# Scores of split f16 pairs from half the array's rows, without stacked copies, and a third input buffer

## The chip, the cores and the metric

The kernel runs on one core of one Trainium2 chip. A core has a matrix engine (TensorE, PE in the profile, with its weight loads shown apart as PEld), a vector engine (VectorE, DVE), a scalar engine (ScalarE, ACT), a general engine (GpSimd, POOL), and a queue engine (SyncE, SP) that here issues nearly all transfers. The metric is the device time of one execution in microseconds, the median of several.

## What is computed

```python
# q, k, v: (8, 12, 448, 64); w_in: (768, 2048); w_out: (2048, 768); all float32
scores = q @ k.T / sqrt(64) - log(448)
attn   = 1 / (1 + exp(-scores))            # sigmoid, no row sums
x      = attn @ v                          # heads side by side: (3584, 768)
h      = x @ w_in
g      = where(h >= 1, h, where(h <= -1, 0, (h + 1)**2 / 4))
out    = g @ w_out
```

## The kernel before

The work is cut by batch (8 of them, 448 tokens each). In a batch the 12 heads make 6 pairs of heads, so there are 48 pairs, counted p = 0 to 47. The two heads of a pair lie in partitions 0 to 63 and 64 to 127, since a head is 64 wide. A pair's keys are cut into chunks of 128: three whole ones and a last one of 64, in which both heads share one tile (`mid` in the code).

**Pairs and their formats.** Pairs 0 to 7 are computed in float32 straight from the input. From pair 8 on, q and k are split into a high and a low f16 part (from pair 14 on v and the sigmoids too), and a score is the sum of three terms: high by high, low k by high q, high k by low q. A pair passes these steps: `load_pair` transfers its q, k and v into a tile `raw` (704 KB, lines 304 to 321); `prep_a` lets ACT sum absolute values of q, k and v for a scale (line 337; the tile `dump` receives what nobody reads); `all_sum` adds the sums over partitions (line 154 and a small matmul, line 157); `prep_b` makes scales on DVE and splits the tile, on POOL from pair 17 on, into `hl` (for q and k, each high and low) and `v` (lines 373 to 375). The last reader of a `raw` tile is the split of its v on line 375.

**The stacked copy.** `prep_b` then copies `hl` into a tile `qk` by 8 transfers of 56 KB: for each head, high q stands twice, in rows 0 to 63 and 64 to 127, and high k above low k. A matmul over all 128 rows (line 443) then gives the first two terms of one head at once; the third term is a matmul over a head's own 64 rows (line 458). The transfers go through SP's queue, which is in order, and each waits for the part of the split that it copies. The last chunk of pairs 14 and later is done otherwise, by three matmuls with a block of `corner` weights (line 436).

**The rest of attention.** ACT makes the sigmoid in place (line 487), ACT and DVE split it (lines 495 and 496), and PE multiplies with v (line 533). The result of the pair is taken from PSUM by ACT (line 542), its largest value by DVE (line 543).

**The two products.** Batches 0 and 1 use plain f16 splits of `w_in` (line 761). From batch 2 on the product with `w_in` is done in blocks with seven products in place of eight (line 727), with sums in between on ACT and DVE (lines 739, 736 and 745). `bend` makes g: ACT (line 774), DVE twice (775 and 776), ACT writes the high part of g to `ghl` (777), DVE the low part (778). The product with `w_out` (line 797) reads `ghl`, chunk by chunk; its tile `po` is scaled by DVE (line 810) and stored. `load_set` (line 703) brings the next blocks of weights. I call the first product of a batch the up blocks and the second the down products. The g of the last up block is ready only some time after PE has gone on to the down products.

**Order.** The attention of batch b + 1 is woven into the products of batch b: `step(i)` handles a chunk, and its first chunk of a pair p calls `load_pair(p + 3)` and `prep_a(p + 2)`, its third chunk `prep_b(p + 2)` and, from pair 14 on, `prep_a(p + 3)`. The program text gives priorities only; a scheduler with a simulated timeline puts each engine's instructions in order, and each engine then works in that order and waits at the first instruction that isn't ready. The tile `raw` has two buffers, so pair p + 3 can be loaded only when pair p + 1 has been split.

```python
        if c == 0:
            load_pair(p + 3)
            prep_a(p + 2)
        if c == 2:
            prep_b(p + 2)
            if late:
                prep_a(p + 3)
```

Of the kernel before, what the change touches and what calls it, by code (L numbers as in the profile page):

```python
# [14 lines left out]
F32 = mybir.dt.float32  # L15
F16 = mybir.dt.float16
# [7 lines left out]
P = 128  # L24
# [7 lines left out]
NFULL = 8  # L32
NHALF = 6
# [38 lines left out]
def sigmoid_attention_mlp(ctx: ExitStack, tc: tile.TileContext, first_qvk, qkv, w_in, w_out, out_t):  # L72
    nc = tc.nc
    NFULL, _, _, S = first_qvk.shape
# [3 lines left out]
    D = P // 2  # L78
    VW = S + D
    NKC = S // P  # L80
    NPC = NKC + 1
# [5 lines left out]
    raw_p = ctx.enter_context(tc.tile_pool(name="raw", bufs=2))  # L87
    stk_p = ctx.enter_context(tc.tile_pool(name="stk", bufs=2))
# [31 lines left out]
    rows = xhl.rearrange("p c h n -> p (c h n)").bitcast(F32)  # L120
    blocks = drm_p.tile([NFC // 2, P, SET], F16, name="blocks")

    def scales(m, n, tag, pool=None, square=False, less=0):
# [24 lines left out]
        out=ident, in_=ident, pattern=[[-1, P]], compare_op=ALU.is_equal, fill=0.0, base=0, channel_multiplier=1  # L148
# [136 lines left out]
    raws, maxes, ready, hls, sums = {}, {}, {}, {}, {}  # L285
# [7 lines left out]
    def slot_of(p):  # L293

        return (p + 2) % NFB
# [8 lines left out]
    def load_pair(p):  # L304
        if p >= NPAIR or not first_time("load", p):
            return
        if p < NFULL:
            r = full[:, slot_of(p)]
            nc.sync.dma_start(out=r[:, ::2, :], in_=first_qvk[p, :, ::2, :])
            nc.sync.dma_start(out=r[:, 1, :], in_=first_qvk[p, :, 1, :])  # L310
            ready[p] = r, r[:, 1]
            return
        src = qkv[p - NFULL]
        raws[p] = raw_p.tile([P, 2 * S + VW], F32, tag="raw", name="raw")
        if p < NFULL + NHALF:
            v = stk_p.tile([P, VW], F32, tag="v", name="v", bufs=3)
            nc.sync.dma_start(out=raws[p][:, : 2 * S], in_=src[:, : 2 * S])
            nc.sync.dma_start(out=v, in_=src[:, 2 * S :])
            ready[p] = v
        else:  # L320
            nc.sync.dma_start(out=raws[p], in_=src)
# [22 lines left out]
    def prep_b(p):  # L344
        if not NFULL <= p < NPAIR or not first_time("split", p):
            return
        r, m = raws.pop(p), maxes.pop(p)
        n = 2 if p < NFULL + NHALF else 3
        m = sums.pop(p) if p in sums else all_sum(m, n)

        s, inv = scales(m, n, "qkv")
        sqk = sml_p.tile([P, 2], F32, tag="sqk", name="sqk")
        if n == 3:
            nc.vector.tensor_scalar(out=sqk[:, 1:2], in0=inv[:, 2:3], scalar1=1.0 / ATT, scalar2=None, op0=ALU.mult)
        nc.vector.tensor_scalar(
            out=sqk[:, 0:1], in0=inv[:, 0:1], scalar1=inv[:, 1:2], scalar2=1.0 / math.sqrt(D), op0=ALU.mult, op1=ALU.mult
        )
        hl = hls.pop(p, None) or stk_p.tile([P, 2, 2, S], F16, tag="hl", name="hl")
        parts = [hl[:, 0], hl[:, 1]]
        if n == 3:  # L360
            v = stk_p.tile([P, 2, VW], F16, tag="v", name="v", bufs=3)
            parts.append(v)
        else:
            v = ready[p]
        for t, dst in enumerate(parts):
            rt, hi = r[:, t * S : 2 * S + VW if t == 2 else (t + 1) * S], dst[:, 0, :]
            if p < QA and t != QT:
                nc.scalar.activation(hi, rt, AF.Copy, scale=s[:, t : t + 1])
                nc.vector.scalar_tensor_tensor(  # L369
                    out=dst[:, 1, :], in0=rt, scalar=s[:, t : t + 1], in1=hi, op0=ALU.mult, op1=ALU.subtract  # L370
                )
                continue
            nc.gpsimd.tensor_scalar(out=rt, in0=rt, scalar1=s[:, t : t + 1], scalar2=1.0, op0=ALU.mult, op1=ALU.mult)  # L373
            nc.gpsimd.tensor_scalar(out=hi, in0=rt, scalar1=1.0, scalar2=1.0, op0=ALU.mult, op1=ALU.mult)
            nc.gpsimd.tensor_tensor(out=dst[:, 1, :], in0=rt, in1=hi, op=ALU.subtract)  # L375

        qk = stk_p.tile([P, 2, 2, S], F16, tag="qk", name="qk")
        for j in range(2):
            src = slice(j * D, (j + 1) * D)
            for h in range(2):  # L380
                dst = slice(h * D, (h + 1) * D)
                nc.sync.dma_start(out=qk[dst, j, 0], in_=hl[src, 0, 0, :])
                nc.sync.dma_start(out=qk[dst, j, 1], in_=hl[src, 1, h, :])
        ready[p] = qk, v, sqk, inv, hl

    pieces = {}

# [16 lines left out]
    def chain():  # L404

        begun = []

        def run(issue):
            if not begun:
                begun.append(issue())  # L410
                return
            with tc.high_priority(offset=RUN_PRIO):
                tc.keep_in_program_order(issue())

        return run

    def scores(todo):

        tiles = []
        for i in todo:  # L420
            p, c = divmod(i, NPC)
            mid = c == NKC
            w = slice(c * P, S if mid else (c + 1) * P)
            psc = ps_sc.tile([P, 2, 512], F32, tag="psc", name="psc")
            tiles.append(psc)
            run = chain()
            if p < NFULL:
                r = ready[p][0]
                for j in range(2):
                    out = psc[j * D : (j + 1) * D, 0, :S] if mid else psc[:, j, :S]  # L430
                    rows = slice(j * D, (j + 1) * D)
                    run(lambda: nc.tensor.matmul(out, r[rows, 2, w], r[rows, 0, :], start=True, stop=True))
            elif mid and p >= NFULL + NHALF:
                hl = ready[p][4]
                for t, (kh, qh) in enumerate(((0, 0), (1, 0), (0, 1))):
                    run(lambda: nc.tensor.matmul(
                        psc[:, 0, :S], corner(p)[:, kh, :], hl[:, 0, qh, :], start=t == 0, stop=t == 2
                    ))
            else:
                kq = ready[p][0]  # L440
                for j in (1, 0):
                    out = psc[j * D : (j + 1) * D, 0, :S] if mid else psc[:, j, :S]
                    run(lambda: nc.tensor.matmul(out, kq[:, j, 1, w], kq[:, j, 0, :], start=True, stop=False))  # L443
        for i, psc in zip(todo, tiles):
            p, c = divmod(i, NPC)
            if c == NKC and p >= NFULL + NHALF and p + 2 in maxes:

                sums[p + 2] = all_sum(maxes[p + 2], 3, psc[:, 1, :])
        for i, psc in zip(todo, tiles):
            p, c = divmod(i, NPC)  # L450
            mid = c == NKC
            if p >= NFULL and not (mid and p >= NFULL + NHALF):
                hl, w = ready[p][4], slice(c * P, S if mid else (c + 1) * P)
                run = chain()
                for j in range(2):
                    rows = slice(j * D, (j + 1) * D)
                    out = psc[rows, 0, :S] if mid else psc[:, j, :S]
                    run(lambda: nc.tensor.matmul(out, hl[rows, 1, 0, w], hl[rows, 0, 1, :], start=False, stop=True))  # L458
        for i, psc in zip(todo, tiles):
            weigh(i, psc)  # L460
        for p, c in (divmod(i, NPC) for i in todo):
            if c == 0 and p >= NFULL + NHALF:
                if p < NFULL + NHALF + 2:
                    nc.gpsimd.memset(corner(p), 0.0)
                for j in range(2):
                    rows = slice(j * D, (j + 1) * D)
                    (nc.vector if p < CORN else nc.gpsimd).tensor_copy(  # L467
                        out=corner(p)[rows, :, rows], in_=ready[p][4][rows, 1, :, NKC * P :]
                    )

    def corner(p):

        return corners[:, p % 2 * 2 * P : (p % 2 + 1) * 2 * P].rearrange("p (h n) -> p h n", h=2)
# [359 lines left out]
    def step(i):  # L833

        p, c = divmod(i, NPC)
        late = i >= NPC * (NFULL + NHALF)
        if c == 0:
            load_pair(p + 3)
            prep_a(p + 2)
        if c == 2:  # L840
            prep_b(p + 2)
            if late:
                prep_a(p + 3)
        if i < NPC * GROUPED:
            more, some = i + LAG + 1, [i]
        else:

            more, some = i + 4, [i, i + 1]
            if c % 2:
                return  # L850
        more = min(more, B * NPIECE)
        if more > state["scored"]:
            scores(range(state["scored"], more))
            state["scored"] = more
        av(some)
# [155 lines left out]
```

## Time and profile before

| | |
|---|---|
| median of 3 runs | 1168.32 us (1165.77 to 1192.78) |
| the profiled execution | 1167.41 us, of which its span 1165.40 us |
| PE busy | 1124.0 us, 96% |
| DVE busy | 820.0 us, 70% |
| ACT busy | 723.3 us, 62% |
| POOL busy | 295.6 us, 25% |
| transfers | 170.00 MB, of which `qk` 320 of 56 KB each |

The span counts from the first instruction to the last. Busy times of PE are those of overlapping matmuls: a matmul of 448 columns is shown with about 355 ns, but the next one starts 189 ns after it. In the views below, a row of the timeline gives start, duration and engine, then source line, operation, tile written and tiles read, and the count of instructions that were merged; in square brackets stands how long the engine had been idle before it and what ended that. A row of the chain of waits is shorter: start, duration, engine, tile and line. PEclk is the granted share of the matrix engine's clock.

### The profile page before, as it was taken

To read this page: it belongs to the slowest core of one execution; us is meant where nothing else is said; L and a number is where in the kernel's file an instruction comes from. 1 tells how busy PE (TensorE), PEld (TensorE's weight loads), DVE (VectorE), ACT (ScalarE), POOL (GpSimd) and SP (SyncE) were. 2 spreads that over 40 slices of the span, in tenths; PEclk is the share of its full clock that TensorE was granted. 3 is DMA by queue.
4 is the path that set the end of the run, shared out by engine and by line. 5 is a ranking of instruction groups with operands and counts; after the bars stand their busy time and mean duration, and the time that the engine had idled before them with its cause. 6 is when DMAs were issued, how large, how long until landed. Compare 5 with 4: busy or idle time off the path is not lost.

```text
span 1165.4 us, 20217 instructions
## 1 busy us (share of the span) xinstructions
PE 1124.0 (96%) x7662; PEld 670.0 (57%) x7662; DVE 820.0 (70%) x1730; ACT 723.3 (62%) x1199; POOL 295.6 (25%) x367
## 2 busy tenths in 40 slices
PE   8899999999999999999999998999999998999998
PEld 2234334544446874577645875467845676558954
DVE  6988877778877993569835897268954689636820
ACT  6978887568758884568644786448854576423410
POOL 0000000001552362325432443415354233310000
PEclk9999999999999999999999999999999999999999
DMA  9943442252555654235622464214733064302300
GB/s 361 381 138 138 158 150 88 58 199 88 202 186 188 246 195 134 65 131 207 214 65 65 140 239 166 75 55 158 271 128 100 28 235 146 109 24 105 150 19 30
DMA packets 58112, 170.00 MB, mean 146 GB/s; under 512 B 8608, under 2 KB 39840, under 8 KB 51872
## 3 DMA queue, kind: packets, MB, share of 16 engines
q1 hardware_dynamic: 56288, 159.29, 39.5%
q10 hardware_dynamic: 1728, 9.44, 2.2%
q8 instruction: 60, 0.98, 0.3%
q14 instruction: 36, 0.29, 0.1%
HBM read 126.94 MB, written 23.40 MB: 129 GB/s over the span
## 4 chain that ended last, share of the span: by engine, by line
PE 65%; DVE 14%; ACT 6%; DMA 5%; POOL 4%; issue 4%; SPq 1%; POOLq 0%; ACTq 0%; DVEq 0%
PE po L797 31%; PE ph L727 14%; PE ph L761 7%; PE pav L533 6%; DMA raw<-qkv 4%; DVE ahl L496 3%; PE psc L443 3%; DVE g L775 2%; DVE g L776 2%; DVE xhl L736 2%; PE psc L458 2%; POOL hl L375 2%; DVE ghl L778 1%; POOL raw L373 1%; DMA w_out_sb<-w_in 1%
## 5 line engine op out<-in xcount | busy, mean ns | idle before, releaser
L797 PE MATMUL po<-ghl,w_out_sb 128*128 128x448 f16 x2304 | 451.9, 355 | 10.7 <-ACT ghl L777 10.2
L797 PEld LDWEIGHTS <-w_out_sb 128*128 128x128 f16 x2304 | 222.8, 98 | 228.9 <-issue 30.5
L727 PE MATMUL ph<-w_in_sb 128*128 128x224 f16 x3024 | 306.7, 260 | 9.8 <-DVE xhl L736 8.6
L727 PEld LDWEIGHTS <-w_in_sb 128*128 128x128 f16 x3024 | 285.7, 98 | 33.0 <-issue 26.5
L496 DVE SCALAR_TENSOR_TENSOR ahl<-psc,ahl 128x896 f16<-128x896 f32 (+1 forms) x170 | 152.8, 899 | 119.1 <-ACT ahl L495 117.5
L487 ACT ACTIVATE psc<-psc,nls,sqk 128x896 f32<-128x896 f32 (+1 forms) x136 | 129.9, 969 | 93.6 <-PE psc L458 57.7
L373 POOL TENSOR_SCALAR raw<-raw,qkv_s 128x448 f32<-128x448 f32 (+1 forms) x93 | 68.6, 752 | 439.8 <-DVE qkv_i L137 248.0
L495 ACT ACTIVATE ahl<-psc 128x896 f16<-128x896 f32 (+1 forms) x170 | 127.9, 762 | 35.1 <-DVE ahl L496 33.3
L761 PE MATMUL ph<-xhl,w_in_sb 128*128 128x448 f16 x576 | 112.5, 353 | 2.1 <-DVE g L776 2.1
L337 ACT ACTIVATE dump<-raw 128x448 f16<-128x448 f32 (+1 forms) x105 | 61.6, 587 | 71.1 <-DMA raw<-qkv 67.0
L778 DVE TENSOR_TENSOR ghl<-g,ghl 128x448 f16<-128x448 f32 x128 | 85.8, 677 | 23.1 <-ACT ghl L777 22.7
L736 DVE TENSOR_TENSOR xhl<-ph,xhl 128x224 f32<-128x224 f32 x240 | 87.1, 382 | 15.9 <-PE ph L727 11.4
L777 ACT ACTIVATE ghl<-g 128x448 f16<-128x448 f32 x128 | 73.2, 573 | 34.3 <-DVE g L776 33.4
L774 ACT ACTIVATE g<-xhl,hr,ihr 128x448 f32<-128x448 f32 x96 | 68.4, 753 | 38.9 <-DVE xhl L736 38.1
L775 DVE SCALAR_TENSOR_TENSOR g<-g,rk 128x448 f32<-128x448 f32 x112 | 85.2, 774 | 9.2 <-ACT g L774 8.8
L761 PEld LDWEIGHTS <-w_in_sb 128*128 128x128 f16 x576 | 54.9, 98 | 59.8 <-issue 9.9
L533 PE MATMUL pav<-ahl,v 128*64 128x448 f16 x748 | 83.7, 357 | 2.3 <-DVE ahl L496 2.3
L375 POOL TENSOR_TENSOR hl<-raw,hl 128x448 f16<-128x448 f32 x62 | 72.8, 1195 | 0.0
L776 DVE SCALAR_TENSOR_TENSOR g<-xhl,ihs,g 128x448 f32<-128x448 f32 x96 | 72.0, 770 | 0.2
L443 PE MATMUL psc<-qk 128*128 128x448 f16 x252 | 65.1, 354 | 2.8 <-ACT a L484 1.6
L810 DVE TENSOR_SCALAR o<-po,od 128x448 f32<-128x448 f32 x42 | 28.5, 678 | 55.2 <-PE po L797 55.1
L467 POOL COPY w_in_sb<-hl 64x128 f16<-64x128 f16 x68 | 32.7, 480 | 134.9 <-DVE hl L369 133.0
(151 smaller groups left out, 1122.7 us busy)
## 6 DMA issues: line engine op xcount, KB each, us to landing
w_in_sb<-blocks SPq DMA_DIRECT2D x48, 1344.0 KB, 6.4
raw<-qkv SPq DMA_DIRECT2D x34, 704.0 KB, 5.0
qk<-hl SPq DMA_DIRECT2D x320, 56.0 KB, 2.0
w_out_sb<-w_in SPq DMA_DIRECT2D x16, 768.0 KB, 11.1
out_t<-o SPq DMA_DIRECT2D x48, 224.0 KB, 1.9
blocks<-mixs SPq DMA_DIRECT2D x8, 768.0 KB, 3.8
w_out_sb<-w_out ACTq DMA_DIRECT2D x6, 768.0 KB, 5.0
raww<-w_out ACTq DMA_DIRECT2D x6, 768.0 KB, 5.3
```

What stands on the lines that cost most here:

```text
L375: nc.gpsimd.tensor_tensor(out=dst[:, 1, :], in0=rt, in1=hi, op=ALU.subtract)
L443: run(lambda: nc.tensor.matmul(out, kq[:, j, 1, w], kq[:, j, 0, :], start=True, stop=False))
L487: nc.scalar.activation(a, a, AF.Sigmoid, bias=nls, scale=sqk)
L495: nc.scalar.activation(hi, x, AF.Copy, scale=ATT)
L496: made.setdefault(i, []).append(nc.vector.scalar_tensor_tensor(out=lo, in0=x, scalar=ATT, in1=hi, op0=ALU.mult, op1=ALU.subtract))
L533: run(lambda: once(nc.tensor.matmul(pav[j * D : (j + 1) * D, :S], *terms[j][t], start=c == 0 and t == 0, stop=mid and t == len(terms[j]) - ...
L727: nc.tensor.matmul(out, w[:, wt, wh, c * P : (c + 1) * P], xc[:, xt, c, xh, :], start=j in (0, 2) and c + wh + xh == 0, stop=c == HC - 1 a ...
L736: add = lambda out, q, other: nc.vector.tensor_tensor(out=out, in0=quarter(q), in1=other, op=ALU.add)
L761: nc.tensor.matmul(ph[:, :S], w_in_sb[:, f, wh, c * P : (c + 1) * P], xhl[:, c, xh, :], start=c == 0 and wh + xh == 0, stop=c == NCC - 1 a ...
L775: nc.vector.scalar_tensor_tensor(out=g, in0=g, scalar=rt, in1=g, op0=ALU.min, op1=ALU.mult)
L778: (nc.gpsimd if f % GPOOL else nc.vector).tensor_tensor(out=ghl[:, f, 1, :], in0=g, in1=hi, op=ALU.subtract)
L797: nc.tensor.matmul(po[:, :S], w_out_sb[:, f, wh, m * P : (m + 1) * P], ghl[:, f, gh, :], start=f == lo and wh + gh == 0, stop=f == hi - 1 ...
```

## The change

The stacked copy is gone, with its tile and its 8 transfers per pair. All three terms of a chunk are matmuls over a head's own 64 rows, straight from `hl`, in six instructions: both heads' first term, both heads' second, both heads' third. The last chunk of pairs 8 to 13 is done likewise with 64 rows and 64 columns; that of later pairs stays with `corner`. `raw` has three buffers in place of two, and from pair 15 on a pair's load is called one pair sooner.

```diff
-        raws[p] = raw_p.tile([P, 2 * S + VW], F32, tag="raw", name="raw")
+        raws[p] = raw_p.tile([P, 2 * S + VW], F32, tag="raw", name="raw", bufs=3)
...
-        qk = stk_p.tile([P, 2, 2, S], F16, tag="qk", name="qk")
-        for j in range(2):
-            src = slice(j * D, (j + 1) * D)
-            for h in range(2):
-                dst = slice(h * D, (h + 1) * D)
-                nc.sync.dma_start(out=qk[dst, j, 0], in_=hl[src, 0, 0, :])
-                nc.sync.dma_start(out=qk[dst, j, 1], in_=hl[src, 1, h, :])
-        ready[p] = qk, v, sqk, inv, hl
+        ready[p] = hl, v, sqk
...
-                kq = ready[p][0]
-                for j in (1, 0):
-                    out = psc[j * D : (j + 1) * D, 0, :S] if mid else psc[:, j, :S]
-                    run(lambda: nc.tensor.matmul(out, kq[:, j, 1, w], kq[:, j, 0, :], start=True, stop=False))
+                hl = ready[p][0]
+                for t, (kh, qh) in enumerate(((0, 0), (1, 0), (0, 1))):
+                    for j in range(2):
+                        rows = slice(j * D, (j + 1) * D)
+                        out = psc[rows, 0, :S] if mid else psc[:, j, :S]
+                        run(lambda: nc.tensor.matmul(
+                            out, hl[rows, 1, kh, w], hl[rows, 0, qh, :], start=t == 0, stop=t == 2
+                        ))
...
-        for i, psc in zip(todo, tiles):
-            p, c = divmod(i, NPC)
-            mid = c == NKC
-            if p >= NFULL and not (mid and p >= NFULL + NHALF):
-                hl, w = ready[p][4], slice(c * P, S if mid else (c + 1) * P)
-                run = chain()
-                for j in range(2):
-                    rows = slice(j * D, (j + 1) * D)
-                    out = psc[rows, 0, :S] if mid else psc[:, j, :S]
-                    run(lambda: nc.tensor.matmul(out, hl[rows, 1, 0, w], hl[rows, 0, 1, :], start=False, stop=True))
...
             load_pair(p + 3)
+            if p + 4 > NFULL + NHALF:
+                load_pair(p + 4)
             prep_a(p + 2)
```

The scheduler makes a new order of it. Two places carry the prediction. The first is SP, in batch 3, around the load that the ACT rows further down wait for. Before, where `raw_6310` is pair 31, `qk_6190<-hl_6179` the copies of pair 29, and `w_in_sb<-blocks` the next weights:

```order
L321 DMA raw_6047<-qkv 128x1408
L703 DMA w_in_sb_90<-blocks_95 128x5376 x2
L382 DMA qk_6190<-hl_6179 64x448
L383 DMA qk_6190<-hl_6179 64x448
L382 DMA qk_6190<-hl_6179 64x448 x2
L383 DMA qk_6190<-hl_6179 64x448 x2
L382 DMA qk_6190<-hl_6179 64x448
L383 DMA qk_6190<-hl_6179 64x448
L321 DMA raw_6310<-qkv 128x1408
L703 DMA w_in_sb_90<-blocks_95 128x5376
L812 DMA out_t<-o_6279 128x448
```

Now, at the same place on SP, where `raw_5990` is pair 31 and `raw_6250` pair 32 (L690 is the old line 703, L799 the old 812):

```order
L321 DMA raw_5697<-qkv 128x1408
L690 DMA w_in_sb_90<-blocks_95 128x5376 x2
L321 DMA raw_5990<-qkv 128x1408
L690 DMA w_in_sb_90<-blocks_95 128x5376 x2
L321 DMA raw_6250<-qkv 128x1408
L690 DMA w_in_sb_90<-blocks_95 128x5376
L799 DMA out_t<-o_6219 128x448
```

The copies are gone, and each load's place holds the next pair: pair 32 now stands where pair 31 stood. Pair 32 takes the third buffer, which pair 29 had; pair 31 took pair 29's buffer before.

The second place is ACT, in the same batch, where the last up blocks' g goes to the first down products. Before, from the last first step of `bend` on (L774) to the writing of `ghl` (L777), with the sums of absolute values of pair 31 (L337):

```order
L774 ACTIVATE g_6272<-xhl_93,hr0_5093,ihr0_5091 128x448
L337 ACTIVATE dump_6430,m3_6429<-raw_6310 128x448
L777 ACTIVATE ghl_94<-g_6266 128x448
L337 ACTIVATE dump_6430,m3_6429<-raw_6310 128x448
L777 ACTIVATE ghl_94<-g_6272 128x448
L487 ACTIVATE psc_6312<-psc_6312,nls_87,sqk_5891 128x2x448
L337 ACTIVATE dump_6430,m3_6429<-raw_6310 128x512
```

Now (L761 is the old line 774, L764 the old 777, L474 the old 487):

```order
L761 ACTIVATE g_6212<-xhl_93,hr0_5045,ihr0_5043 128x448
L337 ACTIVATE dump_6363,m3_6362<-raw_5990 128x448 x2
L337 ACTIVATE dump_6363,m3_6362<-raw_5990 128x512
L764 ACTIVATE ghl_94<-g_6206 128x448
L337 ACTIVATE dump_6562,m3_6561<-raw_6250 128x448
L764 ACTIVATE ghl_94<-g_6212 128x448
L474 ACTIVATE psc_6252<-psc_6252,nls_87,sqk_5839 128x2x448
L337 ACTIVATE dump_6562,m3_6561<-raw_6250 128x448
```

All three sums of pair 31 now stand ahead of both writings of `ghl`, and the first sum of pair 32 stands between the two. The same rows, with the pairs of that batch, stand in batches 2 to 5.

More of the change, by code (lines that the diff above doesn't have):

```diff
@@ L433, in scores @@
             elif mid and p >= NFULL + NHALF:
-                hl = ready[p][4]
+                hl = ready[p][0]
                 for t, (kh, qh) in enumerate(((0, 0), (1, 0), (0, 1))):
@@ L439, in scores @@
             else:
-                kq = ready[p][0]
-                for j in (1, 0):
-                    out = psc[j * D : (j + 1) * D, 0, :S] if mid else psc[:, j, :S]
-                    run(lambda: nc.tensor.matmul(out, kq[:, j, 1, w], kq[:, j, 0, :], start=True, stop=False))
+                hl = ready[p][0]
+                for t, (kh, qh) in enumerate(((0, 0), (1, 0), (0, 1))):
[5 more added lines that the diff above has]
+                        ))
         for i, psc in zip(todo, tiles):
@@ L467, in scores @@
                     (nc.vector if p < CORN else nc.gpsimd).tensor_copy(
-                        out=corner(p)[rows, :, rows], in_=ready[p][4][rows, 1, :, NKC * P :]
+                        out=corner(p)[rows, :, rows], in_=ready[p][0][rows, 1, :, NKC * P :]
                     )
```

## The prediction

> **What bounds the kernel now.** I read the page first, then who waits for whom, then the timeline where the long waits are.
>
> ```profile
> PE 1124.0 (96%) x7662; PEld 670.0 (57%) x7662; DVE 820.0 (70%) x1730; ACT 723.3 (62%) x1199; POOL 295.6 (25%) x367
> PE po L797 <- ACT ghl L777: 10.2, 4, 2.9
> PE ph L727 <- DVE xhl L736: 8.6, 7, 2.6
> ACT dump L337 <- DMA raw<-qkv: 67.0, 15, 7.0
> ```
>
> PE is the bound: of 1165.4 us it idles 41. The waits (total, times, longest) say what a change of inputs can reach. ACT stands still 67.0 us for `raw`, but only what arrives at PE counts. The largest entry there is the down product waiting four times, 10.2 us, for ACT's `ghl`. The timeline of one of the four, in batch 3, tells why (last SP copies and the load, POOL's last split, DVE, ACT, PE, and the transfer from the chain of waits):
>
> ```profile
> 573.28 1.16 POOL L375 TENSOR_TENSOR v<-raw,v 128x512 f16<-128x512 f32 x1
> 574.49 0.60 SPq L383 DMA_DIRECT2D qk<-hl  x1
> 575.19 0.53 SPq L321 DMA_DIRECT2D raw<-qkv  x1
> 575.19 5.12 DMA raw<-qkv
> 576.23 1.27 DVE L776 SCALAR_TENSOR_TENSOR g<-xhl,ihs,g 128x448 f32<-128x448 f32 x2
> 572.82 1.41 ACT L774 ACTIVATE g<-xhl,hr,ihr 128x448 f32<-128x448 f32 x2 [1.00 <-DVE xhl L736]
> 580.39 0.58 ACT L337 ACTIVATE dump<-raw 128x448 f16<-128x448 f32 x1 [6.16 <-DMA raw<-qkv]
> 580.97 0.56 ACT L777 ACTIVATE ghl<-g 128x448 f16<-128x448 f32 x1
> 581.99 0.56 ACT L777 ACTIVATE ghl<-g 128x448 f16<-128x448 f32 x1
> 577.82 2.06 PE L797 MATMUL po<-ghl,w_out_sb 128*128 128x448 f16 x10
> 582.61 8.54 PE L797 MATMUL po<-ghl,w_out_sb 128*128 128x448 f16 x36 [2.72 <-ACT ghl L777]
> ```
>
> Both g are ready on DVE at 576.23 + 1.27 = 577.5, but ACT stands in front of a sum for pair 31, whose `raw` lands at 575.19 + 5.12 = 580.31. It was issued late since it waits for pair 29's split on POOL (end 574.44) and for the last copies. The second `ghl` is there at 582.55, and PE starts at 582.61.
>
> The wait costs more than its length. These are the same 36 products after each of the four waits (chain of waits), and PEclk behind two of them:
>
> ```profile
> 444.53 6.97 PE po L797 x36
> 722.49 8.57 PE po L797 x36
> 861.47 8.65 PE po L797 x36
> 1111.39 50.33 PE po L797 x266
> 444.00:447.00 3.00, 2.47 (x14) 1.28 (x14) 0.91 (x3) 3.00 (x7) 0.00 (x0) 1.00 0.11 39
> 582.00:586.00 4.00, 3.40 (x10) 1.41 (x10) 1.39 (x4) 3.99 (x8) 0.00 (x0) 0.57 0.02 8
> ```
>
> At full clock the 36 take 6.97 us (50.33 / 266 = 0.189 each), after three of the waits 8.54, 8.57 and 8.65: 1.57 + 1.60 + 1.68 = 4.85 us lost to a granted clock of 0.57 over those windows. The Trainium skill ("TensorE: Matmul & The Clock Gate", Why this matters for your kernels) asks for no idle gap over some 3 us; here 2.72 us of idling was enough at 582 and 2.46 was not at 444, so the measured rows decide.
>
> **The scores on PE.** The timeline has both kinds of matmul next to each other, for two chunks and for one:
>
> ```profile
> 507.20 0.92 PE L443 MATMUL psc<-qk 128*128 128x448 f16 x4
> 508.05 0.55 PE L458 MATMUL psc<-hl 64*128 64x448 f16 x4
> 508.53 0.76 PE L533 MATMUL pav<-ahl,v 128*64 128x448 f16 x6
> 513.93 0.54 PE L443 MATMUL psc<-qk 128*128 128x448 f16 x2
> 514.40 0.36 PE L458 MATMUL psc<-hl 64*128 64x448 f16 x2
> 514.70 1.90 PE L727 MATMUL ph<-w_in_sb 128*128 128x224 f16 x18
> ```
>
> Two half-row matmuls take 514.70 - 514.40 = 0.30, four take 508.53 - 508.05 = 0.48. So a second pair of them costs 0.18, as much as one full matmul: the two halves run side by side, and about 0.11 is a change between array shapes. A whole chunk was two full slots and one shared by two halves, three slots; now it is three shared slots, three again. 0.77 us (513.93 to 514.70) stays about 0.77. What grows: the last chunk of pairs 8 to 13, where the two heads' first matmuls had 64 columns each, side by side, goes from two slots to three, 6 x 0.19 = 1.1 us. And by the new order PE changes its array shape 417 times, counted through, where it did 404 times; 13 x 0.1 = 1.3 us. Together +2.4.
>
> **The transfers.** 320 copies leave SP and the DMA engines:
>
> ```profile
> qk<-hl SPq DMA_DIRECT2D x320, 56.0 KB, 2.0
> raw<-qkv SPq DMA_DIRECT2D x34, 704.0 KB, 5.0
> ```
>
> No row of PE's waits names `qk`, so the copies themselves give nothing. What counts is `raw`. One would expect the sums never to wait again, as each load is a pair ahead. The order says otherwise at the four places: pair 31's three sums stand ahead of the `ghl` and find their tile loaded long before; but the scheduler has moved up pair 32's first sum too, between the two `ghl`, and pair 32's load waits for the same split of pair 29, at the same place on SP. On SP only the copies in front are gone. So the load goes out at 574.5 in place of 575.19, lands at 579.6; the sum takes 0.58 and the second `ghl` 0.56, and PE can go on at about 580.9. It arrives at 577.82 + 10 x 0.189 = 579.7. The wait shrinks from 2.9 to 1.2, 1.7 saved, four times: 6.8 us. Pair 31's own sums (1.8 us after 574.23) end before the first g is ready at 576.9, so they cost nothing. Waits of 1.2 us left the clock alone in this trace, for example here (batch 3, up blocks; 36 at 0.096 and a tail make 3.6):
>
> ```profile
> 552.41 3.61 PE L727 MATMUL ph<-w_in_sb 128*128 128x224 f16 x36 [1.06 <-DVE xhl L736]
> 984.99 5.27 PE L727 MATMUL ph<-w_in_sb 128*128 128x224 f16 x36 [1.25 <-DVE xhl L736]
> ```
>
> I count the 4.85 us of clock as saved too. The second row shows the exception: behind several waits in a row the same 36 took 1.66 more. Its waits begin with `raw` of pair 47, which DVE sums itself:
>
> ```profile
> 953.72 0.39 SPq L321 DMA_DIRECT2D raw<-qkv  x1
> 961.35 1.68 DVE L341 TENSOR_REDUCE m<-raw 128x2 f32<-128x896 f32 x2 [3.46 <-DMA raw<-qkv]
> 966.30 1.89 PE L727 MATMUL ph<-w_in_sb 128*128 128x224 f16 x18 [2.61 <-DVE xhl L736]
> ```
>
> Here the new load stands a whole pair earlier on SP and needs the buffer of pair 44, split long before, so the 2.61 us go in full. Of the 1.66 behind it I take half, 0.8 (bounds 0 and 1.66). Two waits around 300 us follow an ACT stopped by `raw`:
>
> ```profile
> 304.58 0.58 ACT L337 ACTIVATE dump<-raw 128x448 f16<-128x448 f32 x1 [1.81 <-DMA raw<-qkv]
> 309.35 1.14 PE L533 MATMUL pav<-ahl,v 128*64 128x448 f16 x10 [1.25 <-DVE ahl L496]
> 325.38 0.58 ACT L337 ACTIVATE dump<-raw 128x448 f16<-128x448 f32 x1 [1.33 <-DMA raw<-qkv]
> 332.99 1.14 PE L533 MATMUL pav<-ahl,v 128*64 128x448 f16 x10 [1.08 <-DVE ahl L496]
> ```
>
> Of 1.25 + 1.08 = 2.3 I take half, 1.2, since mixing of weights fills ACT there too. The new order of everything else has no row. The nearest is the wait of 1.06 at 552.41, which stands in each of four batches: it can go (-4.2) or come twice (+4.2). I see no reason for either side and take 0. SP's waits for a free `raw` stay where they were, so the weight loads and output stores behind them are no later.
>
> The sum: 2.4 - 6.8 - 4.85 - 2.6 - 0.8 - 1.2 = -13.9. From the profiled 1167.41 that is 1153.5; the median lies 0.9 above the profiled execution, so I forecast 1154.
>
> **Rivals.** *The stall stays.* The sum moved up by the scheduler stands in the same line as before; if its transfer takes 1 us longer, or POOL ends pair 29's split 1 us later, the wait at the down products is over 2 us again and the clock drops as at 861.47. Then the 6.8 mostly and the 4.85 are not saved: 1153.5 + 11.7 = about 1165, no change. For it: the same split releases the load. Against: the copies in front are gone, and only one sum stands between.
>
> *Half-row weights don't load ahead* (the side of slower). If the next weights of a half could be loaded only when that half's matmul is done, each following pair of halves pays a weight load.
>
> ```profile
> L458 PEld LDWEIGHTS <-hl x252: 92/92/103, 78.2 to 1023.3; 64*128 64x128 f16 x120, 64*64 64x64 f16 x6
> ```
>
> There are 126 such chunks (120 whole, 6 short) with two following pairs each, 252 x 0.092 = 23.2 us: 1177. It decides from 0.06 us per following pair on, where it eats the 13.9. The Trainium skill ("TensorE: Matmul & The Clock Gate", Part 3, The mechanism) states just this rule: a weight load overlaps matmuls in flight only in other row groups, and here every second load is for the row group that is computing. The four halves at 508.05 speak against it, since their second pair came 0.18 after the first.
>
> *All waits on these chains go.* If landing is quick enough, the left 4 x 1.2 go too, and with them the 1.06 of four batches and the other halves of the small terms: 1154 - 4.8 - 4.2 - 2.0 = 1143.
>
> **How the numbers follow.** The forecast has 0.52, the stall that stays 0.25 (between 1160 and 1168), all waits gone 0.12 (1143 to 1149), weights not ahead 0.07, a new wait of another kind 0.04 (1168 to 1175). By itself the forecast's range is 1149 to 1160. The range 1147 to 1168 leaves out the slow ends and part of the fastest. What can be told from no change in a measurement of this kernel is some 2%, 23 us: under 1145 lies a part of the third case, 0.05; over 1191.7 next to nothing, 0.02; the rest, 0.93, is within.
>
> **What would show it.** ACT's total wait for `raw` falls from 67 us to 10 or 15, with four waits of some 2 us left at the turn to the down products; PE waits for `ghl` there about 1.2 us each, and 36 products take 7.0 after each. Pairs of half-row matmuls start 0.19 apart. DVE's wait for pair 47 is gone. I am wrong if PEclk still falls near 0.57 at those places, if a whole chunk takes over 0.9 us on PE, or if the waits of the up blocks grow.

## The result, and the profile after

| | before | after |
|---|---|---|
| median | 1168.68 us of 4 | 1154.53 us of 4 (1152.82 to 1156.25) |
| the profiled execution | 1167.41 us, span 1165.40 | 1152.84 us, span 1151.1 |
| ratio | | 0.9887 [0.9856, 0.9918] |
| transfers | 170.00 MB | 151.64 MB |

The kernel is 1.1% faster, which is less than the 2% that this measurement tells from no change; the interval alone keeps it under 1. The forecast was 1154. One execution of before (1192.78 us) and one of the first experiment below (1912.69 us) were slow ones; the ratios leave them out, and without them the medians of these two kernels are 1168.32 and 1165.00 us. Line numbers are now 13 lower behind the scores: L784 is the old down product L797, L714 the old up block L727, L764 the old `ghl` L777. L438 are the new scores, L429 is the old `corner` line 436.

The busy times of the page of after come first, and its row for the sums of absolute values on ACT; then the first entry of who waits for whom on PE (total, times, longest, in us):

```profile
PE 1120.0 (97%) x7914; PEld 660.7 (57%) x7914; DVE 831.4 (72%) x1730; ACT 721.2 (63%) x1199; POOL 291.3 (25%) x367
L337 ACT ACTIVATE dump<-raw 128x448 f16<-128x448 f32 (+1 forms) x105 | 61.5, 586 | 2.7 <-DVE mb L154 1.3
PE ph L714 <- DVE xhl L723: 10.5, 6, 3.2
```

ACT's wait for `raw`, 67.0 us before, is gone altogether: 2.7 us of idling are left ahead of its sums, and none of it for a transfer. The down products no longer wait for ACT's `ghl` (10.2 us before). The largest entry left for PE is a wait for DVE. The timeline of after at the turn in batch 3, to be laid beside the one in the prediction (POOL, SP, ACT, PE):

```profile
571.68 1.53 POOL L375 TENSOR_TENSOR v<-raw,v 128x512 f16<-128x512 f32 x1
573.24 0.33 SPq L321 DMA_DIRECT2D raw<-qkv  x1
578.47 0.56 ACT L337 ACTIVATE dump<-raw 128x448 f16<-128x448 f32 x1
579.03 0.56 ACT L764 ACTIVATE ghl<-g 128x448 f16<-128x448 f32 x1
577.24 9.25 PE L784 MATMUL po<-ghl,w_out_sb 128*128 128x448 f16 x48
586.43 1.31 PE L438 MATMUL psc<-hl 64*128 64x448 f16 x12
587.67 1.14 PE L520 MATMUL pav<-ahl,v 128*64 128x448 f16 x10
```

The sum for pair 32 (578.47) stands between the two `ghl`, as the order said. Its tile was loaded from 573.24 on and was there, so it didn't wait; the second `ghl` was written at 579.59, and 48 products ran through without a pause, 9.25 / 48 = 0.19 us each. The granted clock was full (1.00 from 577.2 to 586), and 48 products after each of the other three turns take 9.25 or 9.26 too. The 12 half-row matmuls of two chunks take 587.67 - 586.43 = 1.24 us, six pairs at 0.19 and one change of shape at 0.1.

The new and the grown waits, from PE's timeline of after, with the clock behind the third (columns of the last row: window, us, busy of PE, PEld, DVE, ACT, POOL, PEclk, share of the DMA engines, GB/s):

```profile
551.71 1.88 PE L714 MATMUL ph<-w_in_sb 128*128 128x224 f16 x18 [1.68 <-DVE xhl L723]
553.93 0.73 PE L429 MATMUL psc<-hl,w_in_sb 128*128 128x448 f16 x3 [0.34 <-DVE ahl L483]
292.75 9.79 PE L784 MATMUL po<-ghl,w_out_sb 128*128 128x448 f16 x42 [2.93 <-DVE g L763]
341.88 0.23 PE L173 MATMUL psc<-diag,one 128*128 128x128 bf16 x1 [3.20 <-DVE diag L163]
963.45 3.61 PE L714 MATMUL ph<-w_in_sb 128*128 128x224 f16 x36 [3.16 <-DVE xhl L723]
...
292.80:296.20 3.40, 3.40 (x10) 1.40 (x10) 3.40 (x7) 2.81 (x5) 0.00 (x0) 0.50 0.46 187
```

The first two stand in each of four batches. The single small matmul of line 173 marks the turn from one batch to the next, so it tells where the time went. Its starts, and the ends of the spans, in us:

| kernel | turns of the batches | end |
|---|---|---|
| before | 341.5, 486.0, 625.7, 765.6, 904.6, 1045.3 | 1165.4 |
| after | 341.9, 484.4, 621.1, 757.8, 894.4, 1031.1 | 1151.1 |
| half rows only | 346.7, 491.5, 629.5, 767.2, 904.9, 1044.1 | 1164.4 |
| without the sooner load | 342.1, 487.5, 624.1, 760.8, 897.5, 1035.3 | 1155.4 |
| dead copies | 351.6, 493.8, 630.4, 767.3, 904.0, 1042.3 | 1162.6 |

In the first 342 us nothing was gained. Then each batch but the last is shorter: by 2.0, 3.0, 3.2, 2.4 and 4.0 us. The rows of this table are single, profiled executions.

### The profile page after: what moved, and what is told of

Same layout as the page of the kernel before. It is cut to its first block, busy times and chain, and to the rows that moved or that the text cites. A ratio compares the mean times of both kernels' runs of the same rounds, so it can differ in the third digit from the quotient of the medians.

```text
span 1151.1 us, 20032 instructions
## 1 busy us (share of the span) xinstructions
PE 1120.0 (97%) x7914; PEld 660.7 (57%) x7914; DVE 831.4 (72%) x1730; ACT 721.2 (63%) x1199; POOL 291.3 (25%) x367
## 2 busy tenths in 40 slices
DMA packets 32511, 151.64 MB, mean 132 GB/s; under 512 B 3488, under 2 KB 14240, under 8 KB 26272
## 4 chain that ended last, share of the span: by engine, by line
PE 67%; DVE 20%; ACT 7%; issue 2%; DMA 2%; SPq 0%; DVEq 0%; ACTq 0%
PE po L784 35%; PE ph L714 11%; PE ph L748 8%; PE pav L520 6%; DVE ahl L483 5%; PE psc L438 4%; DVE g L762 4%; DVE g L763 3%; DVE xhl L723 2%; ACT ahl L482 2%; ACT psc L474 2%; DVE ghl L765 1%; PE psc L429 1%; DMA blocks<-mixs 1%; ACT ghl L764 1%
## 5 line engine op out<-in xcount | busy, mean ns | idle before, releaser
L784 PE MATMUL po<-ghl,w_out_sb 128*128 128x448 f16 x2304 | 447.7, 354 | 2.9 <-DVE g L763 2.9
L784 PEld LDWEIGHTS <-w_out_sb 128*128 128x128 f16 x2304 | 222.5, 98 | 220.4 <-issue 19.5
L714 PE MATMUL ph<-w_in_sb 128*128 128x224 f16 x3024 | 303.7, 259 | 10.6 <-DVE xhl L723 10.5
L714 PEld LDWEIGHTS <-w_in_sb 128*128 128x128 f16 x3024 | 284.4, 98 | 37.7 <-issue 36.4
L474 ACT ACTIVATE psc<-psc,nls,sqk 128x896 f32<-128x896 f32 (+1 forms) x136 | 130.3, 971 | 116.6 <-PE psc L438 113.4
L761 ACT ACTIVATE g<-xhl,hr,ihr 128x448 f32<-128x448 f32 x96 | 67.8, 753 | 56.4 <-DVE xhl L723 56.2
L764 ACT ACTIVATE ghl<-g 128x448 f16<-128x448 f32 x128 | 73.2, 572 | 46.5 <-DVE g L763 46.4
L765 DVE TENSOR_TENSOR ghl<-g,ghl 128x448 f16<-128x448 f32 x128 | 91.1, 718 | 11.9 <-ACT ghl L764 11.0
L438 PE MATMUL psc<-hl 64*128 64x448 f16 x756 | 91.3, 352 | 0.3 <-ACT a L471 0.3
L797 DVE TENSOR_SCALAR o<-po,od 128x448 f32<-128x448 f32 x42 | 28.5, 679 | 59.0 <-PE po L784 58.8
L763 DVE SCALAR_TENSOR_TENSOR g<-xhl,ihs,g 128x448 f32<-128x448 f32 x96 | 69.3, 739 | 0.1
L337 ACT ACTIVATE dump<-raw 128x448 f16<-128x448 f32 (+1 forms) x105 | 61.5, 586 | 2.7 <-DVE mb L154 1.3
L454 POOL COPY w_in_sb<-hl 64x128 f16<-64x128 f16 x68 | 27.8, 409 | 129.3 <-DVE hl L369 127.4
```

The lines of the kernel that those rows point to most:

```text
L438: run(lambda: nc.tensor.matmul(out, hl[rows, 1, kh, w], hl[rows, 0, qh, :], start=t == 0, stop=t == 2))
L474: nc.scalar.activation(a, a, AF.Sigmoid, bias=nls, scale=sqk)
L714: nc.tensor.matmul(out, w[:, wt, wh, c * P : (c + 1) * P], xc[:, xt, c, xh, :], start=j in (0, 2) and c + wh + xh == 0, stop=c == HC - 1 a ...
L763: nc.vector.scalar_tensor_tensor(out=g, in0=h, scalar=ihs, in1=g, op0=ALU.mult, op1=ALU.max)
L765: (nc.gpsimd if f % GPOOL else nc.vector).tensor_tensor(out=ghl[:, f, 1, :], in0=g, in1=hi, op=ALU.subtract)
L784: nc.tensor.matmul(po[:, :S], w_out_sb[:, f, wh, m * P : (m + 1) * P], ghl[:, f, gh, :], start=f == lo and wh + gh == 0, stop=f == hi - 1 ...
```

## The experiments

**Half rows only.** The edit, against after:

```diff
-        raws[p] = raw_p.tile([P, 2 * S + VW], F32, tag="raw", name="raw", bufs=3)
+        raws[p] = raw_p.tile([P, 2 * S + VW], F32, tag="raw", name="raw")
...
-            if p + 4 > NFULL + NHALF:
-                load_pair(p + 4)
```

> The half-row scores alone: the copies are gone, the third buffer and the sooner load are not there. Theory A (the gain is the input standing ready when ACT comes to its sums): in its order all three sums of pair 31 stand ahead of both writings of ghl, and the load of pair 31 waits for the split of pair 29 again, so ACT stops for raw at the four turns to the down products, by 2 to 5 us each, PE waits there 1 to 3 us each, and the clock falls behind some of them. At least half of the 14 us is lost: 1160 us or more. Rival B (the gain is the copies being gone from SP and the DMA engines): as the changed kernel, 1153 to 1157 us, ACT's wait for raw under 15 us.

Measured 1165.36 us, 0.9971 [0.9953, 0.9989] of before. From the waits of ACT, and from PE's timeline:

```profile
ACT dump L337 <- DMA raw<-qkv: 48.3, 14, 6.0
587.73 7.13 PE L784 MATMUL po<-ghl,w_out_sb 128*128 128x448 f16 x36 [0.95 <-ACT ghl L764]
558.80 1.89 PE L714 MATMUL ph<-w_in_sb 128*128 128x224 f16 x18 [1.68 <-DVE xhl L723]
293.64 9.48 PE L784 MATMUL po<-ghl,w_out_sb 128*128 128x448 f16 x42 [3.94 <-DVE g L763]
```

In total most of the gain is lost, as expected, but mostly not at the turns, where I had put it. With two buffers, but no copies in front of the loads, the wait at this turn is 0.95 us in place of 2.72 (0.70 to 1.24 at the other three), and 36 products take 7.13 in place of 8.54: the clock doesn't fall, it is 1.00 behind this turn. The three steady batches, those between the second turn and the fifth, take 137.8 us each, 1.7 less than before and 1.1 more than after. Of the 13.3 us between this profile and that of after, 4.8 are lost in the first 347 us, where three waits for DVE (3.94, 2.10 and 3.68 us) stand in the stretch in which DVE mixes weights; 2.3 in the next batch, 3.4 in the three steady ones and 2.6 in the batch with pair 47, where PE waits 3.27 us at 974.84 and the clock falls to 0.60 behind it.

**Without the sooner load.** The third buffer stays:

```diff
             load_pair(p + 3)
-            if p + 4 > NFULL + NHALF:
-                load_pair(p + 4)
```

> The changed kernel with the third buffer, but with the load called where it was called before. Theory A1 (the buffer makes the gain; the scheduler puts the load where the buffer allows it): 1153 to 1157 us, no wait of ACT for raw over 1 us in total. Rival A2 (the sooner call makes it): the load comes half a pair later than in the changed kernel, ACT waits some 2 us at the turns, 1158 us or more.

Measured 1154.97 us, 0.9879 [0.9843, 0.9915], the time of after. Its steady batches take 136.6 to 136.7 us, and ACT has no wait for `raw`. Added to the half rows, the third buffer alone does it; the call a pair sooner adds nothing that can be seen.

**A fourth term.** This kernel computes more than is asked, the product of the two low parts, in two more half-row matmuls per chunk:

```diff
-                for t, (kh, qh) in enumerate(((0, 0), (1, 0), (0, 1))):
+                for t, (kh, qh) in enumerate(((0, 0), (1, 0), (0, 1), (1, 1))):
...
-                            out, hl[rows, 1, kh, w], hl[rows, 0, qh, :], start=t == 0, stop=t == 2
+                            out, hl[rows, 1, kh, w], hl[rows, 0, qh, :], start=t == 0, stop=t == 3
```

> The changed kernel with a fourth pair of half-row matmuls in each chunk, low k by low q, which the reference's accuracy doesn't need: 126 more pairs on PE. Theory C (two halves side by side cost one slot, and their weights load ahead): 126 x 0.19 = 24 us more, 1178 us. Rival D (the weights of a half wait for that half's matmul): 126 x (0.19 + 0.09) = 35 us more, 1189 us. Rival E (the halves run one after the other): 126 x 0.38 = 48 us more, 1202 us.

Measured 1176.82 us, 22.3 over after: 0.18 for each of the 126 new pairs. PE's timeline, first of this kernel and then of after, has the scores of one chunk:

```profile
573.13 0.93 PE L438 MATMUL psc<-hl 64*128 64x448 f16 x8
564.46 1.89 PE L714 MATMUL ph<-w_in_sb 128*128 128x224 f16 x18 [0.38 <-DVE xhl L723]
```

```profile
549.29 0.74 PE L438 MATMUL psc<-hl 64*128 64x448 f16 x6
```

Eight halves take 0.93 where six take 0.74, so a further pair costs 0.19, a matmul's slot and no weight load beside it. The 22.3 are a little less than 126 x 0.19 = 23.9, since the waits changed too. In a steady batch it can be followed: 18 more pairs are 18 x 0.19 = 3.4 us, the wait of the up blocks shrank from 1.68 to 0.38 by the work that now stands in front of it, other waits grew by 0.3, and the batch is 139.2 - 136.7 = 2.5 longer. The rule of the Trainium skill ("TensorE: Matmul & The Clock Gate", Part 3, The mechanism), by which a weight load overlaps only matmuls in other row groups, doesn't hold for these halves. A load of these weights takes 0.092 us, and if it had to wait for the matmul of its own rows, each of these pairs would have cost about 0.28 and not 0.19.

**Dead copies.** The eight copies per pair come back at a quarter of their width, into a tile that nobody reads; the scores don't use it. Copies of full width beside the third buffer weren't tried.

```diff
+        qk = stk_p.tile([P, 2, 2, S // 4], F16, tag="qk", name="qk", bufs=1)
+        for j in range(2):
+            src = slice(j * D, (j + 1) * D)
+            for h in range(2):
+                dst = slice(h * D, (h + 1) * D)
+                nc.sync.dma_start(out=qk[dst, j, 0], in_=hl[src, 0, 0, : S // 4])
+                nc.sync.dma_start(out=qk[dst, j, 1], in_=hl[src, 1, h, : S // 4])
```

> The changed kernel with the 8 copies per pair put back on SP at their old place, a quarter as long (112 of 448 columns, since memory has no room for more) and read by nobody. ACT's order at the turns is that of the changed kernel. Theory A: SP's place in front of the load costs 0.7 to 1.3 us of the load's time, which uses up what is left of the cover at the turns: PE waits 0 to 1.5 us each there, and the clock holds: 1153 to 1160 us. Rival B (the copies in front of the load were the cost): PE's waits of 2 to 3 us and the fallen clock come back at the turns: 1163 us or more.

Measured 1161.96 us, 0.994 [0.9923, 0.9958]: 7.4 over after, between the two theories. The three steady batches are as fast as after's (136.6 to 136.9 us), so three buffers hide these copies at the turns. The profiled execution is the slowest of nine and lies 11.5 us over that of after: 9.7 of it ahead of 352 us, and 1.7 in the batch with pair 47, where the wait of after stands too (3.17 us) but the clock falls behind it (0.57). SP, DVE and PE ahead of 352 us in their timelines, with the transfer from the chain of waits (L661, L678 and L791 are after's L654, L671 and L784):

```profile
289.21 0.47 SPq L383 DMA_DIRECT2D qk<-hl  x1
289.73 0.58 SPq L678 DMA_DIRECT2D blocks<-mixs  x1
289.73 5.56 DMA blocks<-mixs
286.78 1.01 DVE L675 SCALAR_TENSOR_TENSOR mixs<-mixa,mixes,mixs 128x768 f16<-128x768 f32 x1
295.38 1.83 DVE L661 TENSOR_TENSOR mixa<-w_in_sb 128x768 f32<-128x768 f16 x2 [5.10 <-DMA blocks<-mixs]
300.28 10.19 PE L791 MATMUL po<-ghl,w_out_sb 128*128 128x448 f16 x42 [6.62 <-DVE g L770]
```

The mixed weights are ready on DVE at 287.79, but their store goes out at 289.73, behind two copies that wait for POOL's split, and lands 5.56 us later. DVE has to wait for the buffer, and PE for DVE. The same store in after goes out as soon as it is ready and takes 3.27 us:

```profile
281.92 1.01 DVE L668 SCALAR_TENSOR_TENSOR mixs<-mixa,mixes,mixs 128x768 f16<-128x768 f32 x1
282.95 3.27 DMA blocks<-mixs
```

Why the transfer itself took 2.3 us longer wasn't tested; SP issued the other six copies during it. Of the 9.7 us that this kernel is late at the first turn, 6.62 - 2.93 = 3.7 are this longer wait; PE is 3.8 late before it begins already, and that and the rest weren't followed.

**The sum of pair 47 on ACT.** After's largest wait behind 342 us is the one at 963.45, where DVE still sums pair 47. One number moves that to ACT:

```diff
-MAX_ACT = 47
+MAX_ACT = 48
```

> The changed kernel with pair 47's sums of absolute values on ACT like all the others, in place of DVE's largest values (the limit MAX_ACT 48 for 47). Theory F (the wait of 3.2 us at 963 us is DVE's backlog, and the 3.4 us of DVE work of pair 47 are part of it): the wait falls under 2 us, 1151 to 1153 us. Rival G (the backlog comes from POOL working at the same time, which slows DVE's two steps of bend there): the wait stays at 3 us, 1153 to 1156 us.

Measured 1153.44 us, 0.9864 [0.9845, 0.9883]: 1 us under after, within both intervals, so this lowest median of all isn't told from after. In the profiled executions the batch with pair 47 is 1.2 us shorter than after's (135.4 against 136.6), but the first turn comes 1.8 later. The wait shrank as theory F expected, but for the reason of its rival. PE, DVE and POOL at the place in the timeline of this kernel, and then DVE and POOL in that of after:

```profile
963.46 1.89 PE L714 MATMUL ph<-w_in_sb 128*128 128x224 f16 x18 [1.67 <-DVE xhl L723]
959.15 1.63 DVE L762 SCALAR_TENSOR_TENSOR g<-g,rk 128x448 f32<-128x448 f32 x2 [0.35 <-ACT g L761]
960.71 0.97 DVE L763 SCALAR_TENSOR_TENSOR g<-xhl,ihs,g 128x448 f32<-128x448 f32 x1
961.90 0.67 DVE L763 SCALAR_TENSOR_TENSOR g<-xhl,ihs,g 128x448 f32<-128x448 f32 x1
963.02 2.41 POOL L375 TENSOR_TENSOR hl<-raw,hl 128x448 f16<-128x448 f32 x2
965.39 1.15 POOL L375 TENSOR_TENSOR v<-raw,v 128x512 f16<-128x512 f32 x1
```

```profile
939.06 1.67 DVE L341 TENSOR_REDUCE m<-raw 128x2 f32<-128x896 f32 x2
957.35 2.06 DVE L762 SCALAR_TENSOR_TENSOR g<-g,rk 128x448 f32<-128x448 f32 x2 [0.53 <-ACT g L761]
959.34 2.94 DVE L763 SCALAR_TENSOR_TENSOR g<-xhl,ihs,g 128x448 f32<-128x448 f32 x2
957.44 2.86 POOL L375 TENSOR_TENSOR hl<-raw,hl 128x448 f16<-128x448 f32 x2
960.27 1.53 POOL L375 TENSOR_TENSOR v<-raw,v 128x512 f16<-128x512 f32 x1
```

In after, DVE's sum of pair 47 is over at 940.7, long before the wait. But POOL splits the pair sooner there, and the split on line 375 falls together with DVE's rows for g: two of line 763 take 2.94 us there, and 0.97 + 0.67 = 1.64 where POOL comes to line 375 only behind them; with line 762 it is 5.00 against 3.27. These 1.7 us cover the 3.16 - 1.67 = 1.5 by which the waits differ.

**The low part of `ghl` on POOL.** DVE is what PE waits for now. In after all 128 low parts (line 765) are written by DVE; this gives every second one to POOL:

```diff
-GPOOL = 1
+GPOOL = 2
```

> The changed kernel with the low part of g of every second block on POOL in place of DVE (GPOOL 2 for 1). Theory H (PE's waits of 1.7 us in the up blocks are DVE's load alone): 64 x 0.7 us less on DVE, the waits in the up blocks shrink by half, 1148 to 1151 us. Rival G (POOL's work slows DVE when both run, and POOL needs 1.2 us for what takes DVE 0.7): the waits stay or grow and the low part comes later, 1155 to 1170 us.

Measured 1174.56 us, 1.0043 [1.0024, 1.0061]: the rival, and 4.6 us above its range. PE, DVE and POOL at one of the up blocks in its timeline, and the window behind it:

```profile
423.56 3.52 PE L714 MATMUL ph<-w_in_sb 128*128 128x224 f16 x18 [3.31 <-DVE xhl L723]
419.85 1.45 DVE L763 SCALAR_TENSOR_TENSOR g<-xhl,ihs,g 128x448 f32<-128x448 f32 x1
421.52 1.15 DVE L763 SCALAR_TENSOR_TENSOR g<-xhl,ihs,g 128x448 f32<-128x448 f32 x1
419.43 2.77 POOL L375 TENSOR_TENSOR hl<-raw,hl 128x448 f16<-128x448 f32 x2
414.15 1.04 POOL L765 TENSOR_TENSOR ghl<-g,ghl 128x448 f16<-128x448 f32 x1 [1.17 <-ACT ghl L764]
414.34 0.86 DVE L131 TENSOR_SCALAR qkv_e<-qkv_e 128x3 int32<-128x3 int32 x1
...
423.60:427.00 3.40, 3.40 (x19) 2.69 (x19) 2.19 (x4) 2.48 (x7) 1.01 (x3) 0.50 0.64 204
```

The low parts on POOL hold DVE up: the row of three numbers on line 131, 0.16 us elsewhere, lasts 0.86, to the end of POOL's low part beside it, and a row for g beside another low part takes 1.29 (412.17). POOL's split then meets DVE's next rows for g, and these take 1.45 and 1.15. The wait of the up blocks is 3.31 in place of 1.68, and the granted clock is at half behind it. A steady batch is 3.3 us longer than after's; its parts weren't followed further.

**Mixing from other places.** The mixing of weights on DVE is spread over the chunks from `MIX0` to `MIX1`; two kernels move it, to take the waits at 292.75 and 341.88 away:

```diff
-MIX0 = 24
-MIX1 = 96
+MIX0 = 12
+MIX1 = 92
```

> The changed kernel with the eight mixings of weights of batch 1 spread from unit 12 to 92 of 120 in place of 24 to 96. Theory J (what is left in the first 342 us are PE's waits of 2.9 us at 293 and 3.2 us at 342, both behind DVE's mixing, with falls of the clock): with the mixing less dense and over sooner both shrink, batch 2's weights are there in time, 1147 to 1152 us. Rival K (the mixing waits for its own stores on SP and for the first product's splits, so earlier calls only move the waits): 1153 to 1158 us.

```diff
-MIX0 = 24
-MIX1 = 96
+MIX0 = 16
+MIX1 = 88
```

> As the run before, from unit 16 to 88: as dense as in the changed kernel, only 8 units (about 9 us) sooner. Theory J: the wait at 342 us goes, the one at 293 stays, 1149 to 1153 us. Rival K: 1153 to 1158 us.

Measured 1157.87 us, 0.9903 [0.9881, 0.9925], and 1158.55 us, 0.9909 [0.989, 0.9927]: both 3 to 4 us over after, the side of the rival. In the profiled executions both are some 4.8 us late at the first turn, and their steady batches are as long as after's. The wait at 341.88 shrank to 1.4 in the first and went in the second, as meant. The one at the down products grew from 2.9 to 6.1 and to 4.2, and the second has a new one of 2.15 at 294.42, also for DVE. Where the mixing stands decides which of these waits is long, and neither place is better than the old one.

## Why the prediction was right, and where its terms were off

The medians give, step by step: half rows without the copies 1168.3 to 1165.0, -3.3; the third buffer -10.0 more; the sooner call -0.4, which is nothing. At the turns the two halves of the change overlap. A steady batch takes 139.5 us before, 137.8 with the copies gone and two buffers, and 136.7 with three buffers, whether short copies are there or not: without the copies most of the cost of the turns is gone, and with the third buffer all of it. By stretches, from the turns of the batches above, the forecast's terms and the profiled executions stand so (the 1.3 us for changes of shape, spread over all, left out):

| stretch | terms of the forecast, us | measured, us |
|---|---|---|
| first 342 us | +1.1 - 1.2 = -0.1 | +0.4 |
| batch with the first turn | -1.7 | -2.0 |
| the three batches with a turn and a fall of the clock | 3 x -1.7 - 4.85 = -9.95 | -3.0 - 3.2 - 2.4 = -8.6 |
| batch with pair 47 | -2.6 - 0.8 = -3.4 | -4.0 |
| the last | 0 | -0.1 |

- **The scores on PE.** The mechanism holds: pairs of halves start 0.19 apart, and a further pair costs 0.18 to 0.19. The rival of weights that don't load ahead (1177) is refuted by the fourth term. The change of shape, 0.1, fits the 1.24 us of 12 halves; the +2.4 by themselves can't be read out of the total.
- **The turns, 4 x 1.7.** Mis-sized: the waits went to 0, not to 1.2 each, so 10.2 were saved there, 3.4 more than I took. The 1.7 was itself some 0.35 too much on the forecast's own terms: it starts from a wait of 2.9, but the four together are 10.2, and with 4 x 1.2 left that is 5.4 and not 6.8. ACT has no wait for `raw` at all, where I had 10 to 15 us left. The forecast had the load issued at 574.5 with PE coming at 577.82; it was issued at 573.24 with PE coming at 577.24, 0.7 sooner against PE, and the median load lands in 4.2 us (5.0 before). Pair 31's sums weren't free for ACT, as I had them: they start at 575.99 and hold the first `ghl` until 578.00, some 0.6 us behind its g, but PE had other products until then. The rival of the stall that stays is refuted, and by half rows only too, where 0.95 us was left at the turn in batch 3.
- **The clock, -4.85.** Right: 9.25 us for 48 products behind each turn.
- **The new order, 0.** This is the term that was off on the other side. The waits of the up blocks, 4.4 us in all four batches before, are now 1.67 or 1.68 and then 0.34 or 0.35 in each, 8.1 in all: +3.6, near the end of the bounds (+4.2). I had named this as a sign of being wrong; it ate what the turns gave beyond the forecast. Half rows only has the same 1.68 and 0.34, so the third buffer isn't its cause. Nor is POOL beside DVE: the two rows for g ahead of this wait take 0.97 and 0.67 us in after (548.96 and 550.15) and took 1.45 and 1.15 before (550.60 and 552.28). What in the new order is, wasn't settled.
- **Pair 47, -2.6 and -0.8.** Right in size, wrong as a sum. I let the 2.61 go in full and named nothing that would be late next. What went was more, and what came was the wait of 3.16 at 963.45. About 1.5 of it are POOL's split beside DVE's rows for g; the other 1.67 stand in the batches before it too.
- **The two waits around 300 us, -1.2.** Both went, and a third of 2.1 that I hadn't counted. But 2.93 came at 292.75 with a fall of the clock, and 3.20 at 341.88, so the stretch gave nothing.

PE's waits in the batch with pair 47, in its timeline of before (the rows at 966.30 and 984.99 stand in the prediction):

```profile
959.67 1.90 PE L727 MATMUL ph<-w_in_sb 128*128 128x224 f16 x18 [0.50 <-DMA w_in_sb<-blocks]
981.24 1.02 PE L727 MATMUL ph<-w_in_sb 128*128 128x224 f16 x9 [0.31 <-DVE xhl L736]
982.90 0.55 PE L443 MATMUL psc<-qk 128*128 128x448 f16 x2 [0.64 <-PE ph L727]
```

With them it is 0.50 + 2.61 + 0.31 + 0.64 + 1.25 of waits and 1.66 of clock, 7.0 us, against 3.16 after: 3.8 less, and 4.0 were measured.

So the total was met by a right mechanism with terms off in both directions. That the 3.4 us which the turns gave beyond the forecast and the 3.6 which the new order took cancel is luck. What the forecast had right was the place of the gain, the turns with their clock.

## What to carry to other kernels

A buffer that lets a load go a step sooner pays where an in-order engine stands in front of work for the busiest engine and waits for that load; look for the instruction that a scheduler put between two others, not for the engine with the longest wait. Small copies on an in-order queue can cost most by what stands behind them, here a store. Once the bound engine waits for a second one, price that engine's instructions by what runs beside them, since their own durations are then part of the wait.

## What the runs showed of the hardware

**DVE slows down beside POOL.** The same instruction of DVE (line 763, 128x448 in f32, reading `xhl` and g) takes 0.67 us at best and 1.45 or more beside POOL's split on line 375, as the rows above show; whether they meet is decided by the order. Its group, of after and then of the kernel with the low part on POOL:

```profile
L763 DVE SCALAR_TENSOR_TENSOR g<-xhl,ihs,g 128x448 f32<-128x448 f32 x96 | 69.3, 739 | 0.1
```

```profile
L763 DVE SCALAR_TENSOR_TENSOR g<-xhl,ihs,g 128x448 f32<-128x448 f32 x96 | 82.7, 875 | 0.3
```

A mean of 739 or 875 ns for one and the same work is 13 us of DVE over 96 instructions. The Trainium skill ("Trainium Architecture — The Big Picture", What this means for kernel authors) says that these two engines share a pair of ports to the memory under an exclusive lock. The trace agrees in that both are longer when they meet (line 375 on `v` takes 1.53 beside line 763, and 1.15 with pair 47 on ACT). One row fits a lock outright: with the low part on POOL, the three numbers of line 131 take 0.86 or 0.87 us in four batches, and end 0.01 to 0.03 after POOL's low part (414.34 + 0.86 = 415.20, and 414.15 + 1.04 = 415.19). Line 483, which reads one input from PSUM, isn't slowed: it takes 1.08 at 552.71 in after, beside POOL's split, and at most 1.09 anywhere.

**A fall of the clock isn't settled by the length of the wait.** In the kernel before the clock stayed up behind the wait of 2.46 us at 444.53 (36 products in 6.97, in the prediction), but fell behind a shorter one, which the forecast didn't set beside it (timeline of before):

```profile
861.47 8.65 PE L797 MATMUL po<-ghl,w_out_sb 128*128 128x448 f16 x36 [2.10 <-ACT ghl L777]
```

The granted clock was 0.60 from 861.5 to 865.5. Nor does the same wait always do the same. The kernel without the sooner load has nearly the same waits as after: 3.32 at 342.10 where after has 3.20 at 341.88, and 3.16 at 966.46 where after has it at 963.45. The windows behind these two, of that kernel and then of after:

```profile
342.20:348.00 5.80, 5.80 (x17) 2.38 (x18) 5.37 (x20) 3.66 (x6) 0.00 (x0) 0.51 0.34 136
966.50:970.00 3.50, 3.50 (x24) 2.95 (x24) 2.63 (x6) 1.76 (x2) 0.00 (x0) 0.63 0.00 0
```

```profile
341.90:345.30 3.40, 3.40 (x19) 1.81 (x20) 3.29 (x6) 1.17 (x2) 0.00 (x0) 1.00 0.04 14
963.50:967.00 3.50, 3.50 (x37) 3.50 (x37) 3.50 (x7) 2.66 (x4) 0.00 (x0) 1.00 0.26 46
```

In one execution the clock was at half for nearly 6 us and fell again at 966 (0.63 over 3.5 us), in the other it was full at both. This is the likely reason why single executions of after lie at 1152.8 us, with a mean granted clock of 0.998, or at 1156.2, with 0.995. Those without the sooner load part in the same way: 1152.4 and 1153.4 at 0.999, 1156.6 and 1157.1 at 0.995 and 0.994. At which waits the clock fell in the executions that weren't profiled is not on record. A wait of 2 to 3 us on PE thus costs its length each time, and the clock only sometimes.
